# Weights from double to float32: one scaled and shifted word instead of split fields, in a fused attention and Fourier-mixing kernel

## The chip, the cores and the metric

The kernel runs on one core of a Trainium2 chip. A core has five engines that work side by side, each through its own queue in order: TensorE (PE) multiplies matrices out of SBUF into PSUM, VectorE (DVE) and ScalarE (ACT) do elementwise work, GpSimd (POOL) does elementwise work on SBUF only, and SyncE (SP) issues most DMA transfers. They wait for each other through semaphores. The metric is the device time of one execution in microseconds; the median of three runs of the kernel before is 1980.62 us.

## The reference, cut to what matters

Eight batches, each with eight heads of 576 tokens and 64 channels. The attention keeps the 32 largest scores of each row; its output, heads side by side, is x of 576 x 512. Then comes a Fourier mix over tokens and channels, and two matrix products with a relu between them on a normalised sum:

```python
scores = scale * np.matmul(q, k.transpose(0, 1, 3, 2))
kth = np.partition(scores, -top_k, axis=-1)[..., -top_k:-top_k + 1]
scores = np.where(scores >= kth, scores, -1000000000.0)
attn = np.exp(scores - np.max(scores, axis=-1, keepdims=True))
attn = attn / (np.sum(attn, axis=-1, keepdims=True) + 1e-09)
x = np.matmul(attn, v)                      # then (B, H, S, D) -> (B, S, H*D)
u = x + np.real(np.fft.fft(np.fft.fft(x, axis=1), axis=2))
un = (u - mu) / np.sqrt(var + 1e-06)        # mu, var over the channels
out = u + np.maximum(un @ w_ch1, 0.0) @ w_ch2
```

The two weight matrices (512 x 2048 and 2048 x 512) reach the device as 64-bit floating-point numbers, 16 MB in all. [...] the kernel makes float32 of them from their two 32-bit words. That conversion is what changes.

## The kernel before, in words

**Attention in steps.** The work of the attention is a list of 288 items: 32 pairs of heads, nine items each (four full query tiles for each of two heads, and one 64-row tile that holds the remaining rows of both). A Python loop over steps writes the order of every engine by hand. In step i, scores for item i + 3 are computed (`scores`, TensorE L333 and L303, copied out of PSUM by ScalarE, L336 and L307), VectorE finds the 32nd largest value of item i and begins item i + 1 (`top_ops`: MAX8, L354, and MATCH_REPLACE8, L356; four and three of them a step), GpSimd turns the result into two bounds (`bounds`, L363), ScalarE takes a relu (L370), GpSimd subtracts (L371), ScalarE takes the exponential (`expo`, L377), TensorE transposes (`transposes`, L398, L409), ScalarE copies the transposes out (L401, L410), and TensorE multiplies with v (`attend`, L435) when the query tiles of a chunk are there. The two steps of the relu and the exponential are tied by the GpSimd subtract between them.

**Batch 0.** During the first 36 steps there is no other large work for TensorE, since the Fourier mix and the products of a batch come after its attention. The weights are converted in these steps. In this stage relu and subtract of item i stand at the end of step i, the exponential of item i at the head of step i + 1, right after what the plan has under "convert".

**Later batches.** From then on the matrix products of batch b (`hidden`, L741, and `back`, L765) are laid between the attention steps of batch b + 1 by a planner that keeps estimated costs of TensorE; weight conversion has no cost in it.

**The weights.** `weight_chunks` cuts both matrices into 32 chunks of 128 x 512. `weight_steps` gives the functions for a chunk, and `start_of` puts chunk n at step 34 n / 32. A chunk's raw words lie in a slot of `sp1` (three slots, each with room for the words and one more field). The low word is at even, the high word at odd positions. In the kernel before:

- `load` (L158): a DMA of 512 KB into a slot; load n + 3 is issued when chunk n is joined.
- `split` (L167, L170, VectorE, end of step s0): the mantissa bits and the exponent bits of the high word, into two PSUM tiles of the pool `ps_m` (three buffers).
- `convert` part 0 (L182, L184, ScalarE, head of step s0 + 1, between relu and exp): the mantissa field to a float32 from 1 to 2, and the power of two, built as an integer by a relu with the bias `ebias`, so that its bits are those of a float32.
- `convert` part 1 (L188, L189, ScalarE, the place "convert2", after exp and a copy of the scores): the low word as a small float32, and the sign of the high word.
- `join` (L197, GpSimd): add the low part (place "join", before the subtract of the same step), then multiply with the sign and with the power of two (place "pool", after the subtract).

When the first weight matrix is there, its columns are centred (`centre`: TensorE L906, copy L919, GpSimd subtract L915, four for each of four column groups; the first two groups in steps of batch 0).

Of the kernel before, what the change touches and what calls it, by code (L numbers as in the profile page):

```python
# [9 lines left out]
F32 = mybir.dt.float32  # L10
I32 = mybir.dt.int32
U32 = mybir.dt.uint32
AF = mybir.ActivationFunctionType
ALU = mybir.AluOpType
# [4 lines left out]
P = 128  # L19
# [45 lines left out]
def kernel(  # L65
# [9 lines left out]
    nc = tc.nc  # L75
# [3 lines left out]
    scale = 1.0 / float(D) ** 0.5  # L79
# [25 lines left out]
    const = ctx.enter_context(tc.tile_pool(name="const", bufs=1))  # L105
# [6 lines left out]
    ps_m = ctx.enter_context(tc.tile_pool(name="ps_m", bufs=3, space=bass.MemoryType.PSUM))  # L112
# [7 lines left out]
    mv = [const.tile([P, 5, 2], F32, name=f"mv{i}", tag=f"mv{i}") for i in range(2)]  # L120
    den_t = [const.tile([P, 10], F32, name=f"den{i}", tag=f"den{i}") for i in range(3)]
    cc = const.tile([P, 2], F32, name="cc", tag="cc")
    ebias = const.tile([P, 1], F32, name="ebias", tag="ebias")
    nat_t = const.tile([P, NC, 2, D], F32, name="nat", tag="nat")

    kt_t = const.tile([P, P], F32, name="kt", tag="kt")
# [8 lines left out]

    def weight_chunks(dst, src, n, wc):
        return [
            (dst[:, t, c:c + wc], src[P * t:P * (t + 1), c:c + wc])  # L140
            for t in range(n) for c in range(0, dst.shape[2], wc)
        ]

    def weight_steps(chunks, space, wc, slots):

        fields = {}

        def words(n):
            o = 3 * wc * (n % slots)
            return space[:, o:o + 2 * wc], space[:, o + 2 * wc:o + 3 * wc]  # L150

        def load(n):
            if n < len(chunks):
                dst, src = chunks[n]
                if moe_w_ch1.dtype == F32:
                    nc.sync.dma_start(out=dst, in_=src)
                else:
                    nc.sync.dma_start(out=words(n)[0].bitcast(I32), in_=src.bitcast(I32))  # L158

        def split(n):  # L160
            if moe_w_ch1.dtype == F32:
                return
            high = words(n)[0][:, 1:2 * wc:2].bitcast(I32)
            fields[n] = [
                ps_m.tile([P, wc], I32, name=f"{name}_{n}", tag="mm") for name in ("wm", "we")
            ]
            nc.vector.tensor_scalar(  # L167
                out=fields[n][0], in0=high, scalar1=0xFFFFF, scalar2=None, op0=ALU.bitwise_and
            )
            nc.vector.tensor_scalar(  # L170
                out=fields[n][1], in0=high, scalar1=20, scalar2=0x7FF,
                op0=ALU.logical_shift_right, op1=ALU.bitwise_and,
            )

        def convert(n, part):
            if moe_w_ch1.dtype == F32:
                return
            raw, ex = words(n)
            dst, low, high = chunks[n][0], raw[:, 0:2 * wc:2], raw[:, 1:2 * wc:2]
            if part == 0:  # L180
                m, e = fields.pop(n)
                nc.scalar.activation(out=dst, in_=m, func=AF.Copy, scale=2.0 ** -20, bias=1.0)  # L182

                nc.scalar.activation(  # L184
                    out=ex.bitcast(I32), in_=e, func=AF.Relu, scale=2.0 ** 23, bias=ebias
                )
            else:
                nc.scalar.activation(out=low, in_=low.bitcast(U32), func=AF.Copy, scale=2.0 ** -52)  # L188
                nc.scalar.activation(out=high, in_=high.bitcast(I32), func=AF.Sign)  # L189

        def join(n, parts):
            if moe_w_ch1.dtype == F32:
                return
            raw, ex = words(n)
            dst, low, high = chunks[n][0], raw[:, 0:2 * wc:2], raw[:, 1:2 * wc:2]
            for part in parts:
                nc.gpsimd.tensor_tensor(  # L197
                    out=dst, in0=dst, in1=(low, high, ex)[part],
                    op=ALU.mult if part else ALU.add,
                )  # L200

        return load, split, convert, join


    nat, qT_of, kT_of, v_of, PT, Ssb, Wk, Wp, M8, Nt = ({} for _ in range(10))
# [153 lines left out]
    def bounds(i):  # L359

        if i < N:
            Nt[i] = small.tile([P, 2], F32, name=f"nt_{i}", tag="nt", bufs=6)
            nc.gpsimd.tensor_tensor(  # L363
                out=Nt[i], in0=M8.pop(i)[:, 0:TOPK:TOPK - 1], in1=cc, op=ALU.mult
            )

    def mask(i):

        w = Wk[i]
        nc.scalar.activation(out=w, in_=Ssb[i], func=AF.Relu, scale=-FAR, bias=Nt[i][:, 1:2])  # L370
        nc.gpsimd.tensor_tensor(out=w, in0=Ssb.pop(i), in1=w, op=ALU.subtract)  # L371

    def expo(i):
        pair, t, e = items[i]
        w = Wk[i]
        c = DEN_COL[(t, e)]
        nc.scalar.activation(  # L377
            out=w, in_=w, func=AF.Exp, bias=Nt.pop(i)[:, 0:1],
            accum_out=den_t[pair % 3][:, c:c + 1],
        )  # L380
# [461 lines left out]


    ctx.enter_context(tc.manual_schedule())
    nc.vector.memset(ebias, -896.0 * 2.0 ** 23)

    warm = small.tile([P, 1], F32, name="warm", tag="rd", bufs=6)
    nc.scalar.activation(out=warm, in_=ebias, func=AF.Exp)
    nc.vector.memset(cc[:, 0:1], -1.0)
    nc.vector.memset(cc[:, 1:2], FAR)  # L850
    for t in mv + den_t:
        nc.vector.memset(t, 1.0)
# [18 lines left out]
    def at(step, where, fn, cost=0.0):  # L871
        plan.setdefault((step, where), []).append(fn)
        costs[step] = costs.get(step, 0.0) + cost
# [3 lines left out]
    sp1 = batp.tile([P, NIT * CW[0]], F32, name="space1", tag="hT")  # L877
    WC = 512
    wcs = weight_chunks(w1, moe_w_ch1, NDT, WC) + weight_chunks(w2, moe_w_ch2, NIT, WC)
    n1 = NDT * DF // WC  # L880
    load, split, convert, join = weight_steps(wcs, sp1, WC, 3)
    for n in range(3):
        load(n)
    load_v(0)
# [1 line left out]
    nc.sync.dma_start(out=fs, in_=fs_d.ap())  # L886
    nc.sync.dma_start(out=fd, in_=fd_d.ap())
    nc.sync.dma_start(out=sg, in_=sg_d.ap())
    start_of = [0] + [34 * n // len(wcs) for n in range(1, len(wcs))]
    for n, s0 in enumerate(start_of):  # L890
        at(s0, "dve", lambda n=n: split(n))
        at(s0 + 1, "convert", lambda n=n: convert(n, 0))
        at(s0 + 1, "convert2", lambda n=n: convert(n, 1))
        at(s0 + 1, "join", lambda n=n: join(n, (0,)))
        at(s0 + 1, "pool", lambda n=n: join(n, (1, 2)))
        at(s0 + 1, "load", lambda n=n: load(n + 3))

    ones = batp.tile([P, P], F32, name="ones", tag="yt")
    nc.vector.memset(ones, 1.0 / DM)
# [114 lines left out]
    def run(i, where):  # L1014
        for fn in plan.pop((i, where), []):
            fn()
# [6 lines left out]
    def some(limit):  # L1023

        got = 0.0
        while queue and got + queue[0][0] / 2 <= limit:
            got += one_unit()
        return got
# [6 lines left out]
    i, carry = 0, 0.0  # L1035
    while i < N + 4 or plan or queue:
# [10 lines left out]
        e = items[j][2] if j < N else None  # L1047
# [10 lines left out]
        if pending and pending[0][0] <= i:  # L1058
            _, pp, pc = pending[0]
# [30 lines left out]
        for n, fn in enumerate(fixed):  # L1090
            cost += fn()
            if n == n_mask:
                if PER_BATCH <= i - 1 < N:
                    mask(i - 1)
                run(i, "act")
                run(i, "convert2")
                for fn in out_next:
                    fn()
                out_next.clear()
            if n == min(n_tr, len(fixed) - 1) and PER_BATCH <= i - 1 < N:  # L1100
                expo(i - 1)

            got += some(max(room * (n + 1) / len(fixed) - got, 1.1 if fn in preps else 0.0))
# [27 lines left out]

        run(i, "pool0")
        bounds(i)
        run(i, "join")
        if i < PER_BATCH:
            mask(i)
        for fn in late_now:
# [44 lines left out]
```

## Time and profile before

| | |
|---|---|
| median of three runs | 1980.62 us (1980.1 to 1980.8) |
| profiled span | 1976.8 us |
| busy, whole span | PE 1849.8 us (94%), DVE 1595.5 (81%), ACT 1223.6 (62%), POOL 813.2 (41%) |
| busy, 14 to 260 us | PE 152.3 us of 246, DVE 237.1, ACT 195.3, POOL 192.7; granted TensorE clock 0.76 |
| first transform matmul (`yp`, L598) | at 263.3 us |
| largest shares of the chain that ended last | PE hp L741 24%, PE cp L765 22%, PE o L435 8% |

A line of groups has the source line, engine, operation, what is written from what, shapes and count; then the busy time of all in us, the mean of one in ns, and the idle time of the engine just ahead of them with what ended it. A line of the timeline has the start, the duration and the instruction; the times of instructions that follow each other on one engine overlap a little, so the distance from start to start is shorter than a duration. A line of waits has who waited for whom, the total in us, how many times, and the longest.

### The profile page before, as it was taken

The page shows a single profiled execution, that of the slowest core. Times are in us where ns is not written, and L with a number is a line of the kernel's source. Part 1 is how long each engine was busy: PE and PEld are TensorE (multiplying, and loading weights), DVE is VectorE, ACT ScalarE, POOL GpSimd, SP SyncE. Part 2 cuts the span into 40 slices and gives each one's busy share as a digit, 9 for nine tenths or more (in the row PEclk, how much of TensorE's full clock was granted, in tenths as well). Part 3 has the DMA queues.
Part 4 walks back from the last instruction along what each step waited for, and adds up shares of the span by engine and source line. Part 5 has one row for each costly group of instructions (what it writes and reads, how often), then busy time and mean ns, then how long its engine had stood idle before and what let it go on. Part 6 is the DMA issues. An engine that isn't in the chain of part 4 may idle for free.

```text
span 1976.8 us, 27373 instructions
## 1 busy us (share of the span) xinstructions
PE 1849.8 (94%) x8626; PEld 1120.5 (57%) x8626; DVE 1595.5 (81%) x3273; ACT 1223.6 (62%) x3095; POOL 813.2 (41%) x1088
## 2 busy tenths in 40 slices
PE   5666599999999999999999999999999999998999
PEld 3333356465564656656565656646565656566655
DVE  7999989999899999988889888988889888853000
ACT  6888747776776767666666667666665657641100
POOL 4878834325533364235533454225532454232000
PEclk9777699999999999999999999999999999999999
DMA  4323100011000101010000001010001101000000
GB/s 126 102 84 101 56 7 19 24 27 30 19 19 24 27 24 25 19 32 19 18 24 24 21 16 27 19 32 19 22 20 25 26 13 30 1 14 1 11 14 11
DMA packets 133584, 57.81 MB, mean 29 GB/s; under 512 B 124352, under 2 KB 124480, under 8 KB 133440
## 3 DMA queue, kind: packets, MB, share of 16 engines
q1 hardware_dynamic: 132208, 55.73, 10.6%
q8 instruction: 69, 1.13, 0.2%
q14 instruction: 75, 0.61, 0.1%
q10 hardware_dynamic: 1232, 0.33, 0.1%
HBM read 46.57 MB, written 9.44 MB: 28 GB/s over the span
## 4 chain that ended last, share of the span: by engine, by line
PE 82%; DVE 6%; ACT 5%; POOL 4%; issue 2%; SPq 0%; DMA 0%; POOLq 0%; DVEq 0%; ACTq 0%
PE hp L741 24%; PE cp L765 22%; PE o L435 8%; PE sp L333 6%; PE tpP L398 6%; PE yp L598 3%; PE cp L801 3%; DVE m L354 3%; PE mp L655 2%; DVE wk L356 2%; PE sp_t L303 2%; POOL wk L371 2%; POOL w L197 1%; ACT wk L377 1%; PE tpk L252 1%
## 5 line engine op out<-in xcount | busy, mean ns | idle before, releaser
L371 POOL TENSOR_TENSOR wk<-S,wk 128x576 f32<-128x576 f32 x288 | 407.0, 1413 | 897.1 <-ACT wk L370 845.1
L354 DVE MAX8 m<-wk 128x8 f32<-128x576 f32 x864 | 624.1, 751 | 5.5
L741 PE MATMUL hp<-unT,w 128*128 128x256 f32 (+1 forms) x2048 | 539.6, 410 | 2.5 <-ACT unT L722 2.1
L765 PE MATMUL cp<-w,hT 128*128 128x512 f32 x1024 | 478.4, 599 | 0.0
L741 PEld LDWEIGHTS hp<-unT,w 128*128 128x128 f32 x2048 | 373.5, 190 | 126.7 <-issue 32.5
L356 DVE MATCH_REPLACE8 wk<-m,wk 128x576 f32<-128x576 f32 x576 | 428.1, 743 | 0.0
L765 PEld LDWEIGHTS cp<-w,hT 128*128 128x128 f32 x1024 | 179.3, 190 | 182.3 <-issue 181.5
L377 ACT ACTIVATE wk<-wk,nt 128x576 f32<-128x576 f32 x288 | 225.1, 782 | 67.4 <-POOL wk L371 66.2
L398 PE MATMUL tpP<-ident,wk 128*128 128x128 f32 x1152 | 187.7, 288 | 68.9 <-ACT wk L377 41.4
L401 ACT COPY PT<-tpP 128x512 f32<-128x512 f32 (+1 forms) x320 | 171.1, 545 | 116.7 <-PE tpP L398 114.3
L370 ACT ACTIVATE wk<-S,nt 128x576 f32<-128x576 f32 x288 | 227.0, 788 | 20.0 <-POOL nt L363 18.7
L398 PEld LDWEIGHTS tpP<-ident,wk 128*128 128x128 f32 x1152 | 141.4, 146 | 168.8 <-ACT wk L377 62.1
L354 DVE MAX8 m<-S 128x8 f32<-128x576 f32 x288 | 214.2, 744 | 23.2 <-ACT S L307 22.8
L745 ACT ACTIVATE hT<-hp 128x320 f32<-128x320 f32 (+1 forms) x256 | 104.9, 410 | 196.7 <-PE hp L741 194.5
L356 DVE MATCH_REPLACE8 wk<-m,S 128x576 f32<-128x576 f32 x288 | 214.3, 744 | 0.0
L435 PE MATMUL o<-PT,v 128*64 128x256 f32 (+3 forms) x1440 | 195.8, 414 | 5.0 <-ACT PT L401 4.4
L336 ACT COPY S<-sp 128x512 f32<-128x512 f32 (+1 forms) x264 | 142.0, 589 | 66.6 <-PE sp L333 66.4
L333 PE MATMUL sp<-kT,qT 64*128 64x512 f32 (+1 forms) x528 | 162.3, 675 | 2.4 <-ACT means L919 1.9
L435 PEld LDWEIGHTS o<-PT,v 128*64 128x64 f32 x1440 | 111.4, 153 | 79.1 <-issue 17.4
L197 POOL TENSOR_TENSOR w<-w,space 128x512 f32<-128x512 f32 x96 | 123.7, 1288 | 5.5 <-ACT space L188 2.6
L779 DVE SCALAR_TENSOR_TENSOR x<-cp,gi,x 128x512 f32<-128x512 f32 x11 | 8.2, 746 | 128.3 <-PE cp L765 128.3
L303 PEld LDWEIGHTS sp_t<-kt,qT 128*128 128x128 f32 (+1 forms) x322 | 51.7, 188 | 60.5 <-issue 22.8
(126 smaller groups left out, 1806.0 us busy)
## 6 DMA issues: line engine op xcount, KB each, us to landing
space<-in_moe_w_ch_dram SPq DMA_DIRECT2D x32, 512.0 KB, 3.6
nat<-in_q_dram SPq DMA_DIRECT2D x128, 64.0 KB, 2.1
v<-in_v_dram SPq DMA_DIRECT2D x128, 64.0 KB, 2.1
out_dram<-x SPq DMA_DIRECT2D x32, 256.0 KB, 2.1
nat<-in_k_dram SPq DMA_DIRECT2D x124, 64.0 KB, 2.1
nat<-in_q_dram SPq DMA_DIRECT2D x128, 8.0 KB, 1.7
v<-in_v_dram SPq DMA_DIRECT2D x128, 8.0 KB, 1.7
nat<-in_k_dram SPq DMA_DIRECT2D x124, 8.0 KB, 1.7
```

Source lines behind the costliest of these rows:

```text
L197: nc.gpsimd.tensor_tensor(out=dst, in0=dst, in1=(low, high, ex)[part], op=ALU.mult if part else ALU.add,)
L333: nc.tensor.matmul(sp[r], lhsT=qT[hd, q_cols], rhs=kT[hd, :], start=True, stop=True)
L354: ops.append(lambda src=src, m8=m8: nc.vector.max(out=m8, in_=src))
L356: ops.append(lambda src=src, m8=m8: nc.vector.match_replace(w, m8, src, NEG))
L370: nc.scalar.activation(out=w, in_=Ssb[i], func=AF.Relu, scale=-FAR, bias=Nt[i][:, 1:2])
L371: nc.gpsimd.tensor_tensor(out=w, in0=Ssb.pop(i), in1=w, op=ALU.subtract)
L377: nc.scalar.activation(out=w, in_=w, func=AF.Exp, bias=Nt.pop(i)[:, 0:1], accum_out=den_t[pair % 3][:, c:c + 1],)
L398: nc.tensor.transpose(tp[:, c, :], p_sb[:, k0 + P * c:k0 + P * (c + 1)], ident)
L401: nc.scalar.copy(out=pt[:, NF * he:NF * (he + 1), col:col + w], in_=tp[:, :, o:o + w])
L435: nc.tensor.matmul(o[D * e:D * (e + 1), c0:c1], lhsT=vv[:, c, e, :], rhs=pt[:, 2 * NF if c == NF else NF * e + c, c0:c1], start=(c == 0), ...
L741: nc.tensor.matmul(hp[:, 0:w], lhsT=w1[:, dt, P * it:P * (it + 1)], rhs=unT[:, dt, 0:w], start=(dt == 0), stop=(dt == NDT - 1),)
L765: nc.tensor.matmul(cp, lhsT=hT[:, it, P * n:P * (n + 1)], rhs=w2[:, it, :], start=(it == 0), stop=(it == NIT - 1),)
```

## The change

The double's bits are a sign, eleven bits of exponent and 52 of mantissa. The new version reads the high word as a float32 bit pattern, multiplies that by 2^-112 (ScalarE, into one PSUM tile), and shifts the product's bits left by three (VectorE, into the weight's place): the shift drops the sign and puts exponent and mantissa where a float32 has them, and the factor has set the exponent's offset right. The bits of the low word that still matter, scaled to a whole number, are added to the pattern as integers (GpSimd), and the sign is multiplied on (GpSimd). For each chunk this takes one VectorE operation instead of two, three of ScalarE instead of four and two of GpSimd instead of three. The extra field of a slot is gone, so that the same space holds five slots, and two more loads are issued at the start. ScalarE's three operations all stand between relu and exp; VectorE's shift comes at the end of step s0 + 1 instead of two operations at the end of step s0; both GpSimd operations come after the subtract. The places "convert2" and "join" and the constant `ebias` go.

```diff
-        def split(n):
-            high = words(n)[0][:, 1:2 * wc:2].bitcast(I32)
-            fields[n] = [
-                ps_m.tile([P, wc], I32, name=f"{name}_{n}", tag="mm") for name in ("wm", "we")
-            ]
-            nc.vector.tensor_scalar(
-                out=fields[n][0], in0=high, scalar1=0xFFFFF, scalar2=None, op0=ALU.bitwise_and
-            )
-            nc.vector.tensor_scalar(
-                out=fields[n][1], in0=high, scalar1=20, scalar2=0x7FF,
-                op0=ALU.logical_shift_right, op1=ALU.bitwise_and,
-            )
...
-            if part == 0:
-                m, e = fields.pop(n)
-                nc.scalar.activation(out=dst, in_=m, func=AF.Copy, scale=2.0 ** -20, bias=1.0)
-                nc.scalar.activation(
-                    out=ex.bitcast(I32), in_=e, func=AF.Relu, scale=2.0 ** 23, bias=ebias
-                )
-            else:
-                nc.scalar.activation(out=low, in_=low.bitcast(U32), func=AF.Copy, scale=2.0 ** -52)
-                nc.scalar.activation(out=high, in_=high.bitcast(I32), func=AF.Sign)
...
-            for part in parts:
-                nc.gpsimd.tensor_tensor(
-                    out=dst, in0=dst, in1=(low, high, ex)[part],
-                    op=ALU.mult if part else ALU.add,
-                )
+        def scale_high(n):
+            scaled[n] = ps_m.tile([P, wc], F32, name=f"wh_{n}", tag="mm")
+            nc.scalar.activation(
+                out=scaled[n], in_=words(n)[2], func=AF.Copy, scale=2.0 ** -112
+            )
+        def shift(n):
+            nc.vector.tensor_scalar(
+                out=chunks[n][0].bitcast(I32), in0=scaled.pop(n).bitcast(I32),
+                scalar1=3, scalar2=None, op0=ALU.logical_shift_left,
+            )
+        def rest(n):
+            nc.scalar.activation(
+                out=low.bitcast(I32), in_=low.bitcast(U32), func=AF.Copy, scale=2.0 ** -29
+            )
+            nc.scalar.activation(out=high, in_=high.bitcast(I32), func=AF.Sign)
+        def join(n):
+            bits = dst.bitcast(I32)
+            nc.gpsimd.tensor_tensor(out=bits, in0=bits, in1=low.bitcast(I32), op=ALU.add)
+            nc.gpsimd.tensor_tensor(out=dst, in0=dst, in1=high, op=ALU.mult)
...
-        at(s0, "dve", lambda n=n: split(n))
-        at(s0 + 1, "convert", lambda n=n: convert(n, 0))
-        at(s0 + 1, "convert2", lambda n=n: convert(n, 1))
-        at(s0 + 1, "join", lambda n=n: join(n, (0,)))
-        at(s0 + 1, "pool", lambda n=n: join(n, (1, 2)))
-        at(s0 + 1, "load", lambda n=n: load(n + 3))
+        at(s0 + 1, "convert", lambda n=n: scale_high(n))
+        at(s0 + 1, "convert", lambda n=n: rest(n))
+        at(s0 + 1, "dve", lambda n=n: shift(n))
+        at(s0 + 1, "pool", lambda n=n: join(n))
+        at(s0 + 1, "load", lambda n=n: load(n + AHEAD))
```

More of the change, by code (lines that the diff above doesn't have):

```diff
@@ L122 @@
     cc = const.tile([P, 2], F32, name="cc", tag="cc")
-    ebias = const.tile([P, 1], F32, name="ebias", tag="ebias")
     nat_t = const.tile([P, NC, 2, D], F32, name="nat", tag="nat")
@@ L144, in weight_steps @@
     def weight_steps(chunks, space, wc, slots):
-        fields = {}
+        scaled = {}
         def words(n):
-            o = 3 * wc * (n % slots)
-            return space[:, o:o + 2 * wc], space[:, o + 2 * wc:o + 3 * wc]
+            o = 2 * wc * (n % slots)
+            raw = space[:, o:o + 2 * wc]
+            return raw, raw[:, 0:2 * wc:2], raw[:, 1:2 * wc:2]
         def load(n):
@@ L175, in convert @@
-        def convert(n, part):
+            scaled[n] = ps_m.tile([P, wc], F32, name=f"wh_{n}", tag="mm")
+            nc.scalar.activation(
+                out=scaled[n], in_=words(n)[2], func=AF.Copy, scale=2.0 ** -112
+            )
+        def shift(n):
             if moe_w_ch1.dtype == F32:
                 return
-            raw, ex = words(n)
-            dst, low, high = chunks[n][0], raw[:, 0:2 * wc:2], raw[:, 1:2 * wc:2]
-            if part == 0:
-                m, e = fields.pop(n)
-                nc.scalar.activation(out=dst, in_=m, func=AF.Copy, scale=2.0 ** -20, bias=1.0)
-                nc.scalar.activation(
-                    out=ex.bitcast(I32), in_=e, func=AF.Relu, scale=2.0 ** 23, bias=ebias
-                )
-            else:
-                nc.scalar.activation(out=low, in_=low.bitcast(U32), func=AF.Copy, scale=2.0 ** -52)
-                nc.scalar.activation(out=high, in_=high.bitcast(I32), func=AF.Sign)
@@ L191, in join @@
-        def join(n, parts):
+            nc.vector.tensor_scalar(
[3 more added lines that the diff above has]
+        def rest(n):
             if moe_w_ch1.dtype == F32:
                 return
-            raw, ex = words(n)
-            dst, low, high = chunks[n][0], raw[:, 0:2 * wc:2], raw[:, 1:2 * wc:2]
-            for part in parts:
-                nc.gpsimd.tensor_tensor(
-                    out=dst, in0=dst, in1=(low, high, ex)[part],
-                    op=ALU.mult if part else ALU.add,
-                )
@@ L202, in weight_steps @@
-        return load, split, convert, join
+            _, low, high = words(n)
+            nc.scalar.activation(
[3 more added lines that the diff above has]
+        def join(n):
+            if moe_w_ch1.dtype == F32:
+                return
+            dst, (_, low, high) = chunks[n][0], words(n)
+            bits = dst.bitcast(I32)
+            nc.gpsimd.tensor_tensor(out=bits, in0=bits, in1=low.bitcast(I32), op=ALU.add)
+            nc.gpsimd.tensor_tensor(out=dst, in0=dst, in1=high, op=ALU.mult)
@@ L205 @@
+        return load, scale_high, shift, rest, join
     nat, qT_of, kT_of, v_of, PT, Ssb, Wk, Wp, M8, Nt = ({} for _ in range(10))
@@ L844 @@
     ctx.enter_context(tc.manual_schedule())
-    nc.vector.memset(ebias, -896.0 * 2.0 ** 23)
+    nc.vector.memset(cc[:, 0:1], -1.0)
     warm = small.tile([P, 1], F32, name="warm", tag="rd", bufs=6)
-    nc.scalar.activation(out=warm, in_=ebias, func=AF.Exp)
-    nc.vector.memset(cc[:, 0:1], -1.0)
+    nc.scalar.activation(out=warm, in_=cc[:, 0:1], func=AF.Exp)
     nc.vector.memset(cc[:, 1:2], FAR)
@@ L880 @@
     n1 = NDT * DF // WC
-    load, split, convert, join = weight_steps(wcs, sp1, WC, 3)
+    AHEAD = 5
+    load, scale_high, shift, rest, join = weight_steps(wcs, sp1, WC, AHEAD)
     for n in range(3):
@@ L888 @@
     nc.sync.dma_start(out=sg, in_=sg_d.ap())
+    for n in range(3, AHEAD):
+        load(n)
     start_of = [0] + [34 * n // len(wcs) for n in range(1, len(wcs))]
     for n, s0 in enumerate(start_of):
-        at(s0, "dve", lambda n=n: split(n))
-        at(s0 + 1, "convert", lambda n=n: convert(n, 0))
-        at(s0 + 1, "convert2", lambda n=n: convert(n, 1))
-        at(s0 + 1, "join", lambda n=n: join(n, (0,)))
-        at(s0 + 1, "pool", lambda n=n: join(n, (1, 2)))
-        at(s0 + 1, "load", lambda n=n: load(n + 3))
+        at(s0 + 1, "convert", lambda n=n: scale_high(n))
[3 more added lines that the diff above has]
+        at(s0 + 1, "load", lambda n=n: load(n + AHEAD))
     ones = batp.tile([P, P], F32, name="ones", tag="yt")
@@ L1095 @@
                 run(i, "act")
-                run(i, "convert2")
                 for fn in out_next:
@@ L1133 @@
         bounds(i)
-        run(i, "join")
         if i < PER_BATCH:
```

## The prediction

> **What bounds the kernel now.** The page's second part comes first. It cuts the span into 40 slices of 49.4 us.
>
> ```profile
> PE   5666599999999999999999999999999999998999
> DVE  7999989999899999988889888988889888853000
> PEclk9777699999999999999999999999999999999999
> ```
>
> From the sixth slice on TensorE is at 9 in nearly every slice: it sets the pace. In the first five slices (0 to 250 us, batch 0's attention) TensorE is at 5 or 6, at a granted clock of 0.7, and VectorE is full. All weight conversion lies in this stage: the 32 chunks' instructions run between 20.7 and 240.5 us. So the change is priced there, and what it saves before about 255 us should reach the end whole, because the work after it is TensorE's and stays as it is.
>
> The windows view of the stage has, per row, the stretch, its length, busy time and count of PE, PEld, DVE, ACT, POOL, then clock, DMA share and GB/s:
>
> ```profile
> 100.00:150.00 50.00, 32.27 (x150) 19.55 (x150) 49.52 (x101) 40.28 (x94) 36.42 (x35) 0.74 0.31 92
> 200.00:250.00 50.00, 29.29 (x143) 18.51 (x143) 45.30 (x93) 37.51 (x86) 41.52 (x41) 0.69 0.20 59
> ```
>
> VectorE is busy 49.5 of 50 us up to 150 us, and 45.3 late in the stage, where something else holds too. The waits between 14 and 256 us say how little VectorE stands still:
>
> ```profile
> DVE m L354 <- ACT S L307: 3.8, 4, 2.1
> ```
>
> Next, what conversion costs: groups by shape between 20 and 330 us.
>
> ```profile
> L170 DVE TENSOR_SCALAR we<-space 128x512 int32<-128x512 int32 x32 | 21.9, 686 | 0.0
> L167 DVE TENSOR_SCALAR wm<-space 128x512 int32<-128x512 int32 x32 | 21.9, 685 | 1.5 <-DMA nat<-in_q_dram 1.2 <-ACT w L182 0.4
> ...
> L184 ACT ACTIVATE space<-we,ebias 128x512 int32<-128x512 int32 x32 | 22.0, 689 | 0.0
> L188 ACT ACTIVATE space<-space 128x512 f32<-128x512 uint32 x32 | 21.9, 684 | 0.1
> L189 ACT ACTIVATE space<-space 128x512 f32<-128x512 int32 x32 | 21.4, 670 | 0.0
> L182 ACT ACTIVATE w<-wm 128x512 f32<-128x512 int32 x32 | 19.0, 592 | 3.5 <-DVE wm L167 3.3
> ...
> L197 POOL TENSOR_TENSOR w<-w,space 128x512 f32<-128x512 f32 x96 | 123.7, 1288 | 5.5 <-ACT space L188 2.6 <-PE tpP_t L409 0.4
> ```
>
> That is 2 instructions of VectorE, 4 of ScalarE and 3 of GpSimd per chunk, about one chunk a step. Now one step in the timelines. ScalarE (start, duration):
>
> ```profile
> 102.24 0.79 ACT L370 ACTIVATE wk<-S,nt 128x576 f32<-128x576 f32 x1
> 102.92 0.60 ACT L182 ACTIVATE w<-wm 128x512 f32<-128x512 int32 x1
> 103.39 0.70 ACT L184 ACTIVATE space<-we,ebias 128x512 int32<-128x512 int32 x1
> 104.55 0.78 ACT L377 ACTIVATE wk<-wk,nt 128x576 f32<-128x576 f32 x1 [0.45 <-POOL wk L371]
> ...
> 105.52 0.67 ACT L188 ACTIVATE space<-space 128x512 f32<-128x512 uint32 x1
> 106.08 0.67 ACT L189 ACTIVATE space<-space 128x512 f32<-128x512 int32 x1
> ```
>
> Relu (L370) starts at 102.24, exp (L377) at 104.55; GpSimd's subtract lies between them. Two conversions fill that gap, with 0.45 us left over. The other two (L188, L189) come after exp and cost 0.56 us each, start to start, ahead of the copies out of PSUM. GpSimd where weights are also centred (L915):
>
> ```profile
> 209.03 0.20 POOL L363 TENSOR_TENSOR nt<-m,cc 128x2 f32<-128x2 f32 x1
> 209.17 1.30 POOL L197 TENSOR_TENSOR w<-w,space 128x512 f32<-128x512 f32 x1
> 210.43 1.42 POOL L371 TENSOR_TENSOR wk<-S,wk 128x576 f32<-128x576 f32 x1
> 211.80 2.64 POOL L197 TENSOR_TENSOR w<-w,space 128x512 f32<-128x512 f32 x2
> 214.40 1.27 POOL L915 TENSOR_TENSOR w<-w,means 128x512 f32<-128x512 f32 x1
> ```
>
> No idle time: the next nt comes at 215.63, so such a step is 6.60 us and GpSimd's. Elsewhere VectorE's step is 6.15 us (L167 starts at 20.65, 26.80, 32.94). From nt at 50.02 to nt at 200.96, 23 steps later, the mean is 6.56 us. So three in-order engines are nearly balanced, with VectorE the floor.
>
> **What the Trainium skill says.** "GPSIMD Engine Reference", Engine selection: an add whose three operands are one 32-bit integer type is a native, exact integer add. It gives no price, and no row here shows an integer add. Its section on pitfalls says reads with a byte stride over 8 cost half as much again; these reads have stride 8, and L197 (1288 ns, one operand strided) against L915 (1278 ns, dense) agrees that 8 is free. "ScalarE: Activation LUTs", What ACT_TABLE_LOAD costs: 186 + 0.833 N ns with immediates, 93 more for a pointer operand. For 512 that is 613 and 706 ns; L182 (592) and L184 (689, bias by pointer) agree, L188 and L189 (immediates, SBUF to SBUF, 684 and 670) are slower than it says. "VectorE: DVE Perf Modes", The perf-mode tier table: fp32-wide work touching PSUM runs at one element a cycle, so the shift gets no faster mode; x<-mp (L661), 512 wide out of PSUM, took 693 ns.
>
> **The change part by part.**
>
> VectorE: two tensor_scalars (SBUF to PSUM) become one (PSUM to SBUF). The removed one costs 0.60 us start to start in the chain of waits. The shift: 0.60 if like L167, 0.69 if nothing of it overlaps; I take 0.60 to 0.63. Saving 0.57 to 0.60 x 32 = 18 to 19 us; the step falls from 6.15 to 5.55.
>
> ScalarE: four activations become three, all between relu and exp. The new one reads SBUF and writes PSUM: 592 to 690 ns, 0.47 to 0.56 start to start. Relu's start to the earliest exp is 0.68 + 0.5 + 0.56 + 0.56 = 2.30 us, against the 2.31 that GpSimd's subtract imposes now: the three fit, and exp is not delayed by more than 0.1. After exp 2 x 0.56 = 1.12 us goes. Not all is won: they hid the transposes. After exp (0.87) four transposes at this clock take 1.12 us, and with only two small S copies (0.3) ahead the PT copy waits about 0.8; where two 512-wide S copies (0.96) come first it waits 0.2. So 0.3 to 0.9 is won, 0.6 in the mean. The new shortest ScalarE loop is 2.31 + 0.87 + 1.13 + 0.78 (PT copies) = 5.1 us; four of nine steps carry about 0.9 more (q or k copies, xT and denominators), mean 5.5, and the 64-row tile makes it 5.55. Just under VectorE's 5.55 plus normalising (0.75 in two of nine steps), 5.7.
>
> GpSimd: three operations become two, minus 1.29 us. But the removed add filled the wait for relu, which now shows: 0.20 + 0.7 + 1.41 + 2 x 1.29 = 4.9 us, with centring 6.2 (before 6.60). Bounds of the integer add: 1.29 like the float add, or, as my upper estimate, twice that, 2.6. I take 1.29.
>
> New waits. The shift sits at the end of VectorE's step and waits for ScalarE's wh, written at the head of the same step; behind it queue the next step's MAX8s. VectorE already may not run further ahead than this, because its next MAX8 needs S copied by ScalarE after exp in that step (the 3.8 us above). I cost it at 0 to 3 us. The join waits for the shift, but in its queue stands behind the subtract, which waits for relu: hidden.
>
> Loads, PSUM, setup: five slots instead of three only loosen the loads (VectorE waited 1.2 us once); two loads move 1 MB ahead of pair 1's k, needed five steps later. One PSUM tile per chunk instead of two. Cost nothing. TensorE's order is line for line the same.
>
> Sum: mean step 6.56 to about 5.9 (floor 5.7 plus 0.2 of the 0.3 now lost above the floor): 0.6 x 33 = 20 us. 1980.6 - 20 = 1960.5.
>
> **The rivals.**
>
> (B) ScalarE and TensorE become the bound: with the transposes exposed at clock 0.7, steps with prep or an attend stretch. The waits of transposes for exp (36.6 us in the stage) speak for it, the 5.5 against 5.7 against. Half the gain: 1970.
>
> (C) A slow integer add, 2.6 us: a plain GpSimd step is 6.2 (gain 0.36 x 24 = 8.6), a centring step 7.5 (loss 0.9 x 8 = 7): 1979. For it: no row shows the operation; against: integer addition is no more work than float addition.
>
> (D) Slower: the chain ScalarE to VectorE to GpSimd within a step stalls VectorE, say 0.8 us in each of 32 steps because relu comes 2.7 us after m in some steps (nt 114.59, relu 116.92): +26 - 19, so 1988. Against: wh is needed a whole step later.
>
> **How the numbers follow.** (A) 1960.5 has 0.75, and covers 1953 to 1967: at the low end the 0.3 above the floor and the centring steps' excess (8 x 0.5) vanish as well. (B) 0.14, (C) 0.05, (D) 0.06. The range 1953 to 1973 takes in A and B. Faster 0.91 (A, B and a little of C), same 0.03, slower 0.06.
>
> **What would show it.** Right: 32 VectorE shifts near 0.6 to 0.69 us; VectorE steps near 5.6 to 5.9; exp's wait for GpSimd (19.5 us now) near 0, and PT's wait for transposes (8.1) two or three times as long; integer adds near 1.29; the first yp matmul about 20 us before its 263.3; the rest shifted, not changed. Wrong: an integer add over 2 us, a shift waiting for wh in most steps, or steps still near 6.3 with VectorE idle for S.

## The result and the profile after

The new kernel takes 1956.72 us (median of 4 runs, 1956.37 to 1957.48) against 1980.36 us (4 runs, 1979.19 to 1980.8): a ratio of 0.9882, 95% interval 0.9865 to 0.9899. That is 23.6 us less. The two profiled spans differ by 21.6 us (1976.8 and 1955.2). Between them the first transform matmul (`yp`) moves from 263.2 to 242.2 us, so 21.0 us are gained in batch 0's attention and 0.6 us after it. The other 2 us come from the profiled run of before, which took 1978.57 us, 1.8 less than the median.

The page's 40 slices, 48.9 us each, answer the three rows shown of before:

```profile
PE   6566699999999999999999999999999999998999
DVE  7999989998999989888888879988888879843000
PEclk8787799999999999999999999999999999999999
```

TensorE still waits for the attention in five slices, and its clock there stays at 0.7 to 0.8. The slices that follow look as before. The groups by shape between 20 and 310 us, VectorE, ScalarE and GpSimd in turn, have what replaced the seven rows of before:

```profile
L176 DVE TENSOR_SCALAR w<-wh 128x512 int32<-128x512 int32 x32 | 21.8, 681 | 0.8 <-ACT wh L169 0.8
...
L185 ACT ACTIVATE space<-space 128x512 int32<-128x512 uint32 x32 | 21.2, 663 | 0.0
L188 ACT ACTIVATE space<-space 128x512 f32<-128x512 int32 x32 | 21.2, 661 | 0.0
L169 ACT ACTIVATE wh<-space 128x512 f32<-128x512 f32 x32 | 19.9, 622 | 0.0
...
L195 POOL TENSOR_TENSOR w<-w,space 128x512 int32<-128x512 int32 x32 | 41.3, 1291 | 0.0
L196 POOL TENSOR_TENSOR w<-w,space 128x512 f32<-128x512 f32 x32 | 41.3, 1291 | 2.5
```

Two prices were open: the shift out of PSUM costs 681 ns, and the integer add 1291 ns, exactly what the float multiplication beside it costs. The idle column says that VectorE waited for `wh` 0.8 us in all. ScalarE's timeline for the same item as in the prediction (relu is now L366, exp L373):

```profile
93.12 0.77 ACT L366 ACTIVATE wk<-S,nt 128x576 f32<-128x576 f32 x1 [0.40 <-POOL nt L359]
93.81 0.61 ACT L169 ACTIVATE wh<-space 128x512 f32<-128x512 f32 x1
94.36 0.66 ACT L185 ACTIVATE space<-space 128x512 int32<-128x512 uint32 x1
94.91 0.65 ACT L188 ACTIVATE space<-space 128x512 f32<-128x512 int32 x1
95.47 0.76 ACT L373 ACTIVATE wk<-wk,nt 128x576 f32<-128x576 f32 x1
...
98.21 0.65 ACT L397 COPY PT<-tpP 128x256 f32<-128x256 f32 x2 [0.88 <-PE tpP L394]
...
99.54 0.78 ACT L366 ACTIVATE wk<-S,nt 128x576 f32<-128x576 f32 x1
```

Relu's start to exp's start is 2.35 us (2.31 before), with three conversions in between and no wait in front of exp. From this relu to the next it is 6.42 us; for the same item before it was 7.53 us, from relu at 102.24 to this one:

```profile
109.77 0.77 ACT L370 ACTIVATE wk<-S,nt 128x576 f32<-128x576 f32 x1
```

The copy of the transposes now waits for TensorE, where two conversions stood before. ScalarE's waits between 14 and 234 us:

```profile
ACT PT L397 <- PE tpP L394: 15.1, 24, 1.1
ACT wk L366 <- POOL nt L359: 11.6, 14, 1.8
ACT S L332 <- PE sp L329: 6.2, 6, 1.7
ACT wk L373 <- POOL wk L367: 6.1, 4, 1.5
```

In the same stretch before, exp waited most:

```profile
ACT wk L377 <- POOL wk L371: 14.9, 27, 1.8
ACT PT L401 <- PE tpP L398: 6.5, 8, 1.1
...
ACT wk L370 <- POOL nt L363: 4.1, 6, 1.3
```

GpSimd writes one nt, the bounds, for each item, so from nt to nt is a step. From nt 5 to nt 28 (47.05 to 183.93 us), counted from 0, a step takes 5.95 us in the mean, against 6.56.

### The profile page after: what moved, and what is told of

It is laid out like the page before. It is cut to its first block, busy times and chain, and to the rows that moved or that the text cites. A ratio compares the mean times of both kernels' runs of the same rounds, so it can differ in the third digit from the quotient of the medians.

```text
span 1955.2 us, 27234 instructions
## 1 busy us (share of the span) xinstructions
PE 1842.4 (94%) x8626; PEld 1117.9 (57%) x8626; DVE 1576.6 (81%) x3240; ACT 1202.9 (62%) x3063; POOL 773.3 (40%) x1056
## 4 chain that ended last, share of the span: by engine, by line
PE 80%; DVE 8%; POOL 6%; issue 3%; ACT 2%; DMA 0%; POOLq 0%; SPq 0%; DVEq 0%; ACTq 0%
PE hp L737 24%; PE cp L761 22%; PE o L431 7%; PE tpP L394 6%; PE sp L329 5%; DVE m L350 4%; PE yp L594 3%; DVE wk L352 3%; PE cp L797 3%; PE mp L651 2%; POOL wk L367 2%; PE sp_t L299 2%; POOL w L196 1%; POOL w L195 1%; PE tpk L248 1%
## 5 line engine op out<-in xcount | busy, mean ns | idle before, releaser
L373 ACT ACTIVATE wk<-wk,nt 128x576 f32<-128x576 f32 x288 | 224.8, 781 | 53.5 <-POOL wk L367 52.2
L397 ACT COPY PT<-tpP 128x512 f32<-128x512 f32 (+1 forms) x320 | 171.0, 545 | 124.1 <-PE tpP L394 121.4
L366 ACT ACTIVATE wk<-S,nt 128x576 f32<-128x576 f32 x288 | 226.9, 788 | 27.4 <-POOL nt L359 26.2
L329 PEld LDWEIGHTS sp<-kT,qT 64*128 64x128 f32 (+1 forms) x528 | 42.5, 191 | 61.1 <-issue 44.6
```

The costliest lines, as they stand in the source:

```text
L329: nc.tensor.matmul(sp[r], lhsT=qT[hd, q_cols], rhs=kT[hd, :], start=True, stop=True)
L373: nc.scalar.activation(out=w, in_=w, func=AF.Exp, bias=Nt.pop(i)[:, 0:1], accum_out=den_t[pair % 3][:, c:c + 1],)
L397: nc.scalar.copy(out=pt[:, NF * he:NF * (he + 1), col:col + w], in_=tp[:, :, o:o + w])
```

## The experiments

**What was in question.** The prediction took VectorE's step for the pace of batch 0, with ScalarE's loop just under it. Two theories follow from that. Theory 1: VectorE sets the pace and the others follow, so its 0.60 us a step are the gain. Theory 2: three in-order loops stand so close together that a cut on one engine alone is mostly lost, and the parts of the change are worth something only together. Nine kernels take the parts on and off, alone or in pairs. All times are medians, the ratio is to runs of the kernel before on the same chip (1978.7 to 1980.4 us).

**One part at a time from the kernel before.** One VectorE operation less:

```diff
-            fields[n] = [
-                ps_m.tile([P, wc], I32, name=f"{name}_{n}", tag="mm") for name in ("wm", "we")
-            ]
-            nc.vector.tensor_scalar(
-                out=fields[n][0], in0=high, scalar1=0xFFFFF, scalar2=None, op0=ALU.bitwise_and
-            )
+            fields[n] = [ps_m.tile([P, wc], I32, name=f"we_{n}", tag="mm")] * 2
```

> The kernel before with one VectorE operation less per chunk: the mantissa field is not taken out, and the exponent field stands in for it (the weights are wrong, the other engines' instructions are the same in number and size). Theory 1 (VectorE's step sets batch 0's pace, the other engines follow): the step falls from 6.15 to 5.55 us, 18 to 20 us in all, about 1961. Theory 2 (three in-order loops nearly in balance, so that a cut on one engine alone is mostly lost): ScalarE still has two conversions after exp and GpSimd its 6.6 us steps with centring, so 6 to 12 us, 1968 to 1974.

Measured: 1978.26 us, ratio 0.9994 (0.9985 to 1.0002). Neither theory allowed for so little: 1.8 us, not to be told from nothing. VectorE's waits between 14 and 234 us say where its 19 us went:

```profile
DVE m L349 <- ACT S L302: 11.1, 10, 2.1
DVE we L165 <- DMA space<-in_moe_w_ch_dram: 3.8, 3, 1.7
DVE rd L457 <- ACT rd L456: 3.6, 3, 1.5
DVE we L165 <- ACT wk L365: 2.0, 2, 1.4
DVE x L474 <- PE tpx L470: 1.9, 2, 1.7
```

These are 22.4 us of waiting, against 3.3 in the same stretch of before. What was saved on VectorE has become waiting, half of it for scores that ScalarE has yet to copy. Another 3.8 us are waits for raw words, whose slots come free only when an earlier chunk has been joined.

One GpSimd operation less, by itself and together with the VectorE one:

```diff
-        at(s0 + 1, "pool", lambda n=n: join(n, (1, 2)))
+        at(s0 + 1, "pool", lambda n=n: join(n, (1,)))
```

> The kernel before with two GpSimd operations per chunk instead of three: the multiplication with the power of two is left out (wrong weights). Theory 1: VectorE's floor of 6.15 us a step stays, 0 to 2 us gained, 1978.5 to 1980. Theory 2: the eight steps with centring fall from 6.6 us to VectorE's 6.15, 3 to 5 us gained, 1975.5 to 1977.5.

> Both cuts of the two runs before in one kernel (no mantissa field, no multiplication with the power of two; wrong weights); ScalarE keeps its four operations in the old places. Theory 1: 20 to 22 us, 1958.5 to 1960.5. Theory 2: 10 to 15 us, 1965.5 to 1970.5, and what is missing to the new kernel's 1956.7 is ScalarE's part.

Measured: 1974.18 us (0.9969, 0.9958 to 0.9981) for GpSimd alone, 1972.04 us (0.9960, 0.9945 to 0.9975) for both. GpSimd's part is 5 to 6 us, a little more than expected. The steps with centring are shorter: 6.60 us each before, 5.80, 5.23 and 5.77 with GpSimd's cut alone. But the first `yp` of that run comes only 2.1 us earlier than before (261.1 us), so where the rest arises is not shown. With GpSimd's cut, VectorE's part is still only about 2 us, and both together bring 8 us, less than either theory had. Two thirds of the change's gain are missing, and of the engines' parts only ScalarE's, four operations in the old places, is left.

**ScalarE's places.** The new kernel, with two of its three conversions put back after exp:

```diff
-        at(s0 + 1, "convert", lambda n=n: rest(n))
+        at(s0 + 1, "convert2", lambda n=n: rest(n))
...
                 run(i, "act")
+                run(i, "convert2")
```

> The new kernel with the low word and the sign converted where they were before: after exp and a copy of the scores, not between relu and exp. Same instructions, another order on ScalarE. Theory 1: 0 to 2 us more, 1957 to 1959. Theory 2: ScalarE's loop has its 1.1 us after exp again; the copy of the transposes waits for TensorE less, exp waits for GpSimd again: 6 to 12 us more, 1963 to 1969.

Measured: 1974.21 us (0.9969, 0.9957 to 0.9980), 17.5 us above the new kernel. No instruction differs, only ScalarE's order. It is the largest effect of the study and more than either theory expected. Its waits, 14 to 234 us:

```profile
ACT wk L373 <- POOL wk L367: 32.2, 33, 1.5
...
DVE w L176 <- ACT wh L169: 9.4, 13, 1.3
```

ScalarE now stands idle for a microsecond in nearly every gap between relu and exp (32.2 us, 33 times), and does the same work afterwards in front of the copies; VectorE, for its part, waits for ScalarE. The mean step is 6.54 us.

This led to theory 3: the pace of batch 0 is the longer of two things, VectorE's step and ScalarE's loop from relu to relu. What stands after exp lengthens that loop; what stands between relu and exp hides behind GpSimd's subtract until the gap is full. A test without the new arithmetic: the old four ScalarE operations, all placed in the gap, on the kernel with one VectorE and one GpSimd operation less.

```diff
-        at(s0 + 1, "convert2", lambda n=n: convert(n, 1))
+        at(s0 + 1, "convert", lambda n=n: convert(n, 1))
```

> The run before with one VectorE and one GpSimd operation less (1972.0), and in it all four ScalarE operations between relu and exp instead of two before and two after exp; wrong weights as there. Theory 3 (the pace is the longer of VectorE's step and of ScalarE's loop from relu to relu; what stands after exp lengthens the loop, what stands between relu and exp hides behind GpSimd's subtract until that is full): the four take 0.68 + 0.47 + 0.58 + 0.56 + 0.56 = 2.85 us from relu's start, 0.54 over the subtract's 2.31, against none over with three: about 0.4 us a step above the new kernel, 1965 to 1969. If only the number of operations counted and not their place: 1971 to 1973.

Measured: 1961.73 us (0.9910, 0.9893 to 0.9926), 10.3 us less than with the old places. So place counts, and number counts less than theory 3 had it: four operations in the gap cost 5 us against the new kernel's three, not 8 to 12. Part of that is won back on GpSimd, where this kernel still has its add in front of the subtract, in the wait for relu: against the new kernel its eight steps with centring together take 3.3 us less, and the 23 others between nt 1 and nt 32 take 4.1 us more, 0.18 a step where theory 3 had 0.4. Its timeline in a step with centring:

```profile
205.65 0.21 POOL L358 TENSOR_TENSOR nt<-m,cc 128x2 f32<-128x2 f32 x1
205.79 1.31 POOL L192 TENSOR_TENSOR w<-w,space 128x512 f32<-128x512 f32 x1
207.35 1.41 POOL L366 TENSOR_TENSOR wk<-S,wk 128x576 f32<-128x576 f32 x1 [0.25 <-ACT wk L365]
208.72 1.29 POOL L192 TENSOR_TENSOR w<-w,space 128x512 f32<-128x512 f32 x1
209.97 1.27 POOL L910 TENSOR_TENSOR w<-w,means 128x512 f32<-128x512 f32 x1
211.20 0.19 POOL L358 TENSOR_TENSOR nt<-m,cc 128x2 f32<-128x2 f32 x1
```

From nt to nt 5.55 us. The new kernel does the same number of operations in 6.29:

```profile
191.24 0.19 POOL L359 TENSOR_TENSOR nt<-m,cc 128x2 f32<-128x2 f32 x1
192.32 1.42 POOL L367 TENSOR_TENSOR wk<-S,wk 128x576 f32<-128x576 f32 x1 [0.89 <-ACT wk L366]
193.70 1.28 POOL L195 TENSOR_TENSOR w<-w,space 128x512 int32<-128x512 int32 x1
195.06 1.29 POOL L196 TENSOR_TENSOR w<-w,space 128x512 f32<-128x512 f32 x1
196.31 1.27 POOL L912 TENSOR_TENSOR w<-w,means 128x512 f32<-128x512 f32 x1
197.53 0.19 POOL L359 TENSOR_TENSOR nt<-m,cc 128x2 f32<-128x2 f32 x1
```

Most of the difference of 0.74 us is GpSimd's wait for relu, 0.89 us against 0.25: the add that filled it stands behind the subtract now.

**One cost put back onto the new kernel.** The shift twice; a fourth ScalarE operation after exp; a third GpSimd operation in the old place; no shift at all (ScalarE writes `wh` into the weight's place):

```diff
-            nc.vector.tensor_scalar(
-                out=chunks[n][0].bitcast(I32), in0=scaled.pop(n).bitcast(I32),
-                scalar1=3, scalar2=None, op0=ALU.logical_shift_left,
-            )
+            wh = scaled.pop(n)
+            for _ in range(2):
+                nc.vector.tensor_scalar(
+                    out=chunks[n][0].bitcast(I32), in0=wh.bitcast(I32),
+                    scalar1=3, scalar2=None, op0=ALU.logical_shift_left,
+                )
...
+        def again(n):
+            high = words(n)[2]
+            nc.scalar.activation(out=high, in_=high, func=AF.Sign)
+        at(s0 + 1, "convert2", lambda n=n: again(n))
...
+        def third(n):
+            high, junk = words(n)[2], space[:, 8 * wc:9 * wc]
+            nc.gpsimd.tensor_tensor(out=junk, in0=high, in1=high, op=ALU.add)
+        at(s0 + 1, "join", lambda n=n: third(n))
...
         def scale_high(n):
...
-            scaled[n] = ps_m.tile([P, wc], F32, name=f"wh_{n}", tag="mm")
             nc.scalar.activation(
-                out=scaled[n], in_=words(n)[2], func=AF.Copy, scale=2.0 ** -112
+                out=chunks[n][0], in_=words(n)[2], func=AF.Copy, scale=2.0 ** -112
             )
         def shift(n):
-            nc.vector.tensor_scalar(
-                out=chunks[n][0].bitcast(I32), in0=scaled.pop(n).bitcast(I32),
-                scalar1=3, scalar2=None, op0=ALU.logical_shift_left,
-            )
+            pass
```

> The new kernel with the shift done twice per chunk, from the same source into the same place: one VectorE operation more per chunk, as many as before. Theory 1 (VectorE sets the pace): 0.60 us a step, 18 to 20 us more, about 1976. Theory 2 (loops in balance): the other two loops are now shorter than before, so VectorE's full cost shows as well, but its slack of 0.4 us a step above the floor takes some of it: 13 to 18 us more, 1970 to 1975. A rival in which ScalarE and TensorE set the pace of the new kernel: at most 8 us more, under 1965.

> The new kernel with a fourth ScalarE operation per chunk, after exp and a copy of the scores (the sign taken once more, which changes nothing). 0.56 us of ScalarE in each of 32 steps, 18 us if nothing hides it. Theory 1: 0 to 3 us more, up to 1960. Theory 2: part of it hides the copy's wait for the transposes: 3 to 8 us more, 1960 to 1965. The rival with ScalarE as the pace: 12 to 18 us, 1969 to 1975.

> The new kernel with a third GpSimd operation per chunk in front of the subtract, where the old add was (a sum into a scratch place that nobody reads; four load slots instead of five to make room for it). Theory 1: 0 to 2 us more. Theory 2: plain steps hide it behind relu, the steps with centring go from 6.3 to 6.6 us: 2 to 4 us more, 1959 to 1961.

> The new kernel without the shift: ScalarE writes the scaled word straight into the weight's place and VectorE does nothing for the weights (wrong weights). VectorE's step is 4.95 us of finding maxima. Theory 1: 17 to 19 us less, about 1938. Theory 2: ScalarE's loop of 5.1 to 5.5 us takes over: 5 to 11 us less, 1946 to 1952.

| kernel | us | ratio to before (95%) | to the new kernel | mean step |
|---|---|---|---|---|
| shift twice | 1973.67 | 0.9965 (0.9952 to 0.9978) | +17.0 | 6.39 |
| fourth ScalarE operation after exp | 1964.01 | 0.9918 (0.9903 to 0.9933) | +7.3 | 6.18 |
| third GpSimd operation | 1958.11 | 0.9889 (0.9874 to 0.9904) | +1.4 | 5.94 |
| no shift | 1955.75 | 0.9876 (0.9859 to 0.9892) | -1.0 | 5.93 |

With the shift twice the waits between 14 and 234 us have no row for VectorE, and it is ScalarE that waits, for the bounds:

```profile
ACT wk L368 <- POOL nt L361: 25.2, 21, 2.5
```

Without the shift VectorE waits instead, and the time hardly moves:

```profile
DVE m L346 <- ACT S L299: 17.3, 9, 4.3
```

So VectorE's second operation costs 17 us, its first one 1 us, which is no more than the medians of the kernel before differ between chips. Theory 2 had the first two kernels right and the third a little too dear; that nothing is gained without the shift, neither theory had. In the new kernel VectorE's own work is about 5.8 us a step (6.39, where it never waits, less the 0.60 of a shift), and what else limits the step, ScalarE's loop above all, comes to 5.93: add to VectorE and it leads, take from it and the others do. The fourth ScalarE operation has 18 us of work and costs 7.3, since the copy's wait for the transposes falls from 15.1 to 9.1 us and relu's wait for the bounds from 11.6 to 7.3.

**Load slots.**

```diff
-    AHEAD = 5
+    AHEAD = 3
```

> The new kernel with three slots for raw words and loads three chunks ahead, as before. All theories: the loads land 3.7 us after their issue and a step is 5.9 us, so no difference, within 1 us of 1956.7. If the early loads are part of the gain: 3 us more or above.

Measured: 1956.63 us (0.9887, 0.9872 to 0.9902). No gain from the two extra slots can be seen.

**An attempt to go on.** If transposes that nothing hides now lengthen ScalarE's loop, relu of the next item could go ahead of the copies. In batch 0 the copies and the product with v are held back until relu is issued; only ScalarE's order changes.

In the cut below, `later` holds the copies and `behind` the product with v; they come after relu and ahead of the subtract.

```diff
-    def mask(i):
+    def mask(i, later=()):
...
+        for fn in later:
+            fn()
...
-            mask(i)
+            mask(i, (later or []) + behind)
```

> The new kernel with one more move on ScalarE in batch 0: relu of the next item goes ahead of the copies of the transposes, which then stand between relu and exp too and no longer wait for TensorE in front of relu. The other engines' orders stay. Theory 3: ScalarE's loop loses the exposed wait of 0.5 us and VectorE's 5.55 us plus normalising is the floor: 4 to 8 us less, 1949 to 1953. Rival: the copies come later, TensorE's product with v and the next scores with them, and VectorE waits for S instead: 1956 to 1962.

Measured: 1963.56 us (0.9923, 0.9908 to 0.9938), 6.8 us above the new kernel. That is on the rival's side, though above its range. ScalarE's and TensorE's waits, 14 to 234 us:

```profile
ACT wk L366 <- POOL nt L359: 23.1, 23, 2.2
ACT S L332 <- PE sp L329: 17.8, 11, 2.6
...
PE o L440 <- ACT PT L401: 12.6, 13, 2.4
```

The copies no longer wait for the transposes, but the product with v waits 12.6 us for the copies, the scores queue behind it on TensorE, and ScalarE waits 17.8 us for scores (6.2 before this move). Relu, now in front, waits 23.1 us for the bounds (11.6). The loop runs through TensorE too, and the waits have only changed their place. VectorE waits little, 5.4 us for scores, which the rival had not. The last steps of the stage suffer most: the mean step to nt 28 is 6.06 us, 2.2 us of loss by then, and 8.1 by the first `yp` (250.3 us).

> The run before this one, and batch 0's normalising moved from VectorE (0.75 us, eight times) to ScalarE (about 1.2 us, seven times), as batch 1 has it. If VectorE's step is then the pace: 3 to 6 us less than relu first alone. If ScalarE's loop still is: 2 to 6 us more.

Measured: 1970.04 us (0.9955, 0.994 to 0.997), 6.5 us more again. That looks like ScalarE's loop as the pace, but the run does not show it. VectorE's reciprocal of the sums works in place and now stands behind ScalarE's normalising in the order, so that batch 0's rows are multiplied by the sums and not by their inverses, and VectorE waits until ScalarE has read them (14 to 234 us):

```profile
DVE rd L467 <- ACT x L503: 20.8, 7, 6.4
```

In the run before this one VectorE waited 0.5 us for this reciprocal. Which of the two is the pace stays open for these two kernels.

## Why the prediction was right, and where it was not

**The time and the stage were right.** 1960.5 us was forecast, 1956.7 measured. The step fell to 5.95 us where 5.9 was forecast, steps with centring to 6.29 where 6.2 was. 21.0 us were gained before the first `yp` where 20 were, and what came after moved 0.6 us.

**The prices were right.** The shift, 681 ns and 0.60 us start to start (94.25 to 94.85 in VectorE's timeline); the integer add, 1291 ns, the lower end of its bounds; three conversions in the gap, 2.35 us from relu to exp where 2.30 was forecast. The add's price goes with the Trainium skill, "GPSIMD Engine Reference", Engine selection, which calls the integer add native; the page has no price, and 1291 ns is this case's.

**The waits were nearly right.** VectorE's wait for `wh` is 0.8 us, inside the 0 to 3 allowed, and GpSimd's wait for the shift is hidden (idle 0.0 ahead of L195). PT's wait rose from 6.5 to 15.1 us. Exp's wait fell to 6.1 us and not to nothing: the four that are left average 1.5 us, what an empty gap gives.

**The cause was named only in part.** The step that failed is "VectorE the floor", with the sum built on its 18 to 19 us and ScalarE's loop at "5.5 ... Just under VectorE's". VectorE's cut alone brought 1.8 us, and at the end of its interval 3. The kernel with the shift twice has ScalarE's and GpSimd's parts without VectorE's: it is 6.7 us below the kernel before. The kernel with the old places has VectorE's and GpSimd's parts: 5.8 us. GpSimd's cut by itself brought 5.9. So VectorE's cut and ScalarE's places are each worth next to nothing without the other, and some 17 us with it.

The mean steps fit this. VectorE's own work was about 6.4 us a step (shift twice) and is about 5.8. What else limits the step was 6.54 (old places) to 6.68 (VectorE's cut alone) and is 5.93 (no shift). The pace is the longer of the two, 6.56 before and 5.95 after. That the forecast's number came out is in part luck: both cuts are of about 0.6 us a step, and only one was in its sum.

The prediction added up ScalarE's loop for the new kernel only. Its own estimates, 5.5 and the 0.6 won after exp, give an old loop of 6.1 us, as long as VectorE's 6.15, so that VectorE's cut alone could not pay. The 5.5 was not far off: without the shift, the 23 steps without centring between nt 1 and nt 32 take 5.68 us in the mean, and the eight with centring 6.65, which GpSimd helps to set. The views of waits could not decide it. VectorE's small idle time proves that it was busy, not that it alone set the pace; and of ScalarE's own waits, 39.8 us between 14 and 234 us, 36.5 were for GpSimd and TensorE, which can be slack or links of a loop that goes through these engines.

One contribution is not separated. From nt 1 to nt 32 TensorE's granted clock was 0.73 before and 0.77 after, and the same work took it 121.4 and 117.4 us. As an estimate from these two, a faster TensorE has at most 4 us in the 18 by which these steps became shorter; whether the clock rose because the steps were shorter is not shown.

In rival (D), the 2.7 us from m to relu do not come out of the two times given there (nt and relu), which are 2.33 us apart.

**GpSimd's part** was counted within the slack above the floor. It is 5 to 6 us with the old places on ScalarE, and 1.4 us with the new ones (the third operation put back), no more than the medians of the kernel before differ between chips.

## What to carry to other kernels

An engine with 99% busy time is not for that reason the only one that sets the pace: cut it by itself, and see whether its time falls or only its waits grow. In a chain that goes out to another engine and comes back, put independent work into the gap of the round trip, as much as the gap holds; the same two instructions cost 17.5 us less in the gap than behind exp. One operation too many for the gap cost 5 us there and 7.3 behind exp, in two kernels that differ on GpSimd as well. When two loops are about equally long, expect the smaller of the two cuts, and little from either one alone. So add up every loop for the kernel before as well as for the one after.

## What was not expected of the hardware

- The integer add on GpSimd took 1291 ns for 128 x 512, the same as the float operations beside it, with one operand at a stride of 8 bytes.
- Some VectorE operations were held as long as a GpSimd subtract ran beside them. In the trace of before, a copy of 4 columns (L525, at 258.22 us) takes 1.24 us while the subtract runs from 257.85 to 259.44; its counterpart after, away from the subtract, takes 0.17 us, and there an addition and a subtraction, 128 x 512 each, that meet it (L533, 236.43 us, the subtract from 236.79) take 2.50 us together instead of 1.29. MATCH_REPLACE8 (0.74 us at 93.60, after) and MAX8 (0.75 us at 94.85) keep their times beside the subtract that runs from 93.98 to 95.40. That the two engines share a path to memory is only argued from this; no run tested it.
- Left open: whether the integer add of a chunk, moved one step later into GpSimd's wait for relu, would bring the steps with centring from 6.29 to the 5.55 us seen in the run with four operations in the gap. It was not tried.
